# Attention and MLP on one core: group 0 brought in by strips of tokens, and a second product set between score tiles

## The chip, the cores and the metric

The kernel runs on one core of one Trainium2 chip. The metric is the device time of one execution in microseconds, as the median of several executions. The kernel before takes 394.6 us (three runs, 394.51 to 395.38). "Span" is the time from the first to the last instruction in a profile, some 1.8 us less. All runs used here are fast (one run of the kernel before, of 435.94 us, was slow and is left out).

## The reference

Sigmoid attention on 8 batches of 12 heads (448 tokens, 64 wide), then a two-layer MLP with GELU on the 3584 x 768 result:

```python
scores = scale * np.matmul(q, k.transpose(0, 1, 3, 2)) - np.log(S)
attn = 1.0 / (1.0 + np.exp(-scores))
x = matmul(attn, v)            # then heads side by side: 3584 x 768
h = x @ w_in                   # 768 x 2048
g = 0.5 * h * (1.0 + np.tanh(c * (h + 0.044715 * h * h * h)))
out = g @ w_out                # 2048 x 768
```

## The kernel before

The program is written by a planner: a small simulation in the kernel's source starts operations on each engine when their inputs are ready *by its own estimates*, and the order that results is what the chip executes, with semaphores for the true dependences. So the order of instructions on an engine is fixed once built. If a transfer is later on the chip than in the plan, the engine waits at that place, even if work behind it is ready.

A group is four heads of a batch (24 groups in all). Its q and k (448 KB each) are loaded as fp32, cast to bf16, transposed on TensorE into PSUM and copied to SBUF. Each group has 7 score tiles (four 64x64 matmuls of 448 columns, run at once in the quarters of the array), each followed by a sigmoid on ScalarE, or, after the first 21 tiles, by a tanh on ScalarE and an affine step on VectorE. A second product multiplies the 7 tiles with v (28 matmuls). PSUM has eight banks; a score tile takes a pair of them, a second product takes two, and a group of MLP matmuls takes one.

The planner's choice for TensorE while the MLP has work:

```python
whole = m > 0 and state["avj"] + m == NJ          # all 7 tiles of a group are ready
if pl.pe_mode == 64 and n >= UB and whole and (av_open or banks >= 2):
    ops = av_take(m, t)                           # the second product, right behind a burst
    state["queue"] = ops[1:]
    return ops[0]
size = min(can, banks // 2, free_pairs(t))
if size == BURST or size and hungry or ...:       # BURST = 3 score tiles
    ops = [make_qk(n + x, t) for x in range(size)]
    ...
# else a group of the MLP's first or second layer (make_a, make_b)
```

The loads of group 0 were halves of the partition-major data (`c` = 0, 1), two on SyncE's queue for k and two on ScalarE's for q; GpSimd's queue (v, later groups as bf16, weights) waits for the first half of k:

```python
first[nm] = [plan.add(Op("ld%s0.%d" % (nm, c), "SP" if nm == "k" else "AQ",
                         lambda e, c=c, ap=ap, d=dst[0]: e.dma_start(d[:, c, :], ap[:, c, :]), ...
# casts: k on VectorE, q on ScalarE, one per half; all 7 transposes of k, then of q; copies on both
```

## Time and profile before

| | before |
|---|---|
| device time, median of three | 394.64 us |
| TensorE busy | 98% of 392.7 us |
| first score tile begins | 7.52 us |
| first full MLP group begins ("MLP begins" below) | 29.91 us |
| from there to the end, no wait of TensorE in the records | 362.78 us |

Numbers that no view prints, such as the 362.78, are differences of the starts of single instructions in the same traces.

### The profile page before, as it was taken

The page shows a single profiled execution, that of the slowest core. Times are in us where ns is not written, and L with a number is a line of the kernel's source. Part 1 is how long each engine was busy: PE and PEld are TensorE (multiplying, and loading weights), DVE is VectorE, ACT ScalarE, POOL GpSimd, SP SyncE. Part 2 cuts the span into 40 slices and gives each one's busy share as a digit, 9 for nine tenths or more (in the row PEclk, how much of TensorE's full clock was granted, in tenths as well). Part 3 has the DMA queues.
Part 4 walks back from the last instruction along what each step waited for, and adds up shares of the span by engine and source line. Part 5 has one row for each costly group of instructions (what it writes and reads, how often), then busy time and mean ns, then how long its engine had stood idle before and what let it go on. Part 6 is the DMA issues. An engine that isn't in the chain of part 4 may idle for free.

```text
span 392.7 us, 7379 instructions
## 1 busy us (share of the span) xinstructions
PE 383.5 (98%) x3162; PEld 199.4 (51%) x3162; DVE 142.6 (36%) x243; ACT 237.0 (60%) x366; POOL 50.5 (13%) x82
## 2 busy tenths in 40 slices
PE   7799999999999999999999999999999999999996
PEld 3334455545545454555555555555554555555563
DVE  3347623147635672645443524434432400000000
ACT  5999963588667876857556665565747532333221
POOL 6992110011101201110110100110000000000000
PEclk9999999999999999999999999999999999999999
DMA  8999999657946895895647729637211011111133
GB/s 235 185 201 204 210 203 301 135 143 130 281 85 159 169 240 142 112 242 125 146 109 161 192 14 182 175 68 182 48 42 42 1 42 40 42 40 42 40 82 80
DMA packets 63521, 51.74 MB, mean 132 GB/s; under 512 B 36224, under 2 KB 60032, under 8 KB 63488
## 3 DMA queue, kind: packets, MB, share of 16 engines
q1 hardware_dynamic: 48320, 36.61, 38.3%
q0 software_dynamic: 14528, 13.64, 22.4%
q10 hardware_dynamic: 640, 1.02, 0.7%
q8 instruction: 25, 0.41, 0.4%
q14 instruction: 8, 0.07, 0.1%
HBM read 45.61 MB, written 11.01 MB: 144 GB/s over the span
## 4 chain that ended last, share of the span: by engine, by line
PE 94%; ACT 4%; DMA 1%; issue 0%; DVE 0%; SPq 0%
PE ps L715 38%; PE ps L753 37%; PE ps L581 9%; PE ps L628 8%; ACT at L592 3%; DMA kf<-in_k_dram 1%; PE ps L541 1%; PE ps L538 0%; ACT th L600 0%; ACT L596 0%; PE ps L403 0%; DVE kb L350 0%; ACT ob L349 0%; SPq L454 0%; ACT warm L596 0%
## 5 line engine op out<-in xcount | busy, mean ns | idle before, releaser
L715 PE MATMUL ps<-xT,w_in 128*128 128x448 bf16 x756 | 153.2, 353 | 0.0
L753 PE MATMUL ps<-w_out,gT 128*128 128x384 bf16 x896 | 152.9, 326 | 0.0
L604 DVE TENSOR_SCALAR at<-th 128x896 bf16<-128x896 f32 x147 | 90.5, 625 | 123.0 <-ACT th L600 122.8
L600 ACT ACTIVATE th<-ps 128x896 f32<-128x896 f32 x147 | 127.5, 928 | 0.6 <-PE ps L581 0.6
L753 PEld LDWEIGHTS ps<-w_out,gT 128*128 128x128 bf16 x896 | 86.8, 98 | 62.2 <-issue 2.5
L715 PEld LDWEIGHTS ps<-xT,w_in 128*128 128x128 bf16 x756 | 70.6, 98 | 75.0 <-issue 7.2
L729 ACT ACTIVATE gT<-ps 128x448 bf16<-128x448 f32 x128 | 70.6, 554 | 47.3 <-PE ps L715 47.2
L349 ACT ACTIVATE ob<-ps 128x384 f32<-128x384 f32 x56 | 27.5, 491 | 98.2 <-PE ps L753 98.2
L581 PE MATMUL ps<-qT,kT 64*64 64x448 bf16 x672 | 46.0, 359 | 3.6 <-ACT at L592 3.2
L474 POOL DMA_DIRECT2D vb<-in_v_dram x24 | 14.5, 605 | 213.5 <-PE ps L581 210.5
L628 PE MATMUL ps<-at,vb 64*64 64x448 bf16 x672 | 38.9, 351 | 0.0
L350 DVE CAST xT<-ps 128x448 bf16<-128x448 f32 x42 | 24.5, 619 | 19.8 <-PE ps L628 19.8
L581 PEld LDWEIGHTS ps<-qT,kT 64*64 64x64 bf16 x672 | 15.2, 105 | 30.8 <-issue 14.6
L628 PEld LDWEIGHTS ps<-at,vb 64*64 64x64 bf16 x672 | 20.8, 106 | 13.2 <-issue 7.1
L350 DVE CAST kb<-kf 128x896 bf16<-128x896 f32 (+1 forms) x21 | 13.2, 630 | 15.6 <-DMA kf<-in_k_dram 15.5
L592 ACT ACTIVATE at<-ps 128x896 bf16<-128x896 f32 x21 | 17.4, 935 | 0.8 <-PE ps L581 0.6
L476 POOL DMA_DIRECT2D vb<-in_v_dram x24 | 17.0, 708 | 0.2 <-issue 0.2
L350 DVE CAST qb<-qf 128x896 bf16<-128x896 f32 x19 | 11.9, 625 | 11.7 <-DMA qf<-in_q_dram 11.7
L808 POOL DMA_DIRECT2D w_in<-in_moe_w_in_dram x16 | 9.9, 659 | 0.0
L403 PE MATMUL ps<-gT,ident 128*128 128x512 bf16 x14 | 4.8, 501 | 1.5 <-POOL ident L357 1.5
L350 DVE COPY kT<-ps 128x896 bf16<-128x896 bf16 (+1 forms) x6 | 3.5, 591 | 3.5 <-PE ps L541 1.8
L349 ACT ACTIVATE xT<-ps 128x448 bf16<-128x448 f32 x6 | 3.4, 559 | 1.9 <-PE ps L628 1.9
(30 smaller groups left out, 36.4 us busy)
## 6 DMA issues: line engine op xcount, KB each, us to landing
out_dram<-ob SPq DMA_DIRECT2D x54, 192.0 KB, 2.7
kf<-in_k_dram SPq DMA_DIRECT2D x19, 448.0 KB, 4.3
qf<-in_q_dram SPq DMA_DIRECT2D x18, 448.0 KB, 5.8
vb<-in_v_dram POOLq DMA_DIRECT2D x48, 112.0 KB, 5.4
w_in<-in_moe_w_in_dram POOLq DMA_DIRECT2D x16, 192.0 KB, 10.7
w_out<-in_moe_w_out_dram POOLq DMA_DIRECT2D x4, 768.0 KB, 23.0
kb<-in_k_dram POOLq DMA_DIRECT2D x4, 224.0 KB, 8.6
qb<-in_q_dram POOLq DMA_DIRECT2D x4, 224.0 KB, 9.1
```

The costliest lines, as they stand in the source:

```text
L349: return e.activation(o, i, AF.Copy)
L350: return e.tensor_copy(o, i)
L474: a = plan.add(Op("ldv%da" % g, "SWQ", lambda e, d=dst[0:64], ap=lo: e.dma_start(d, ap), deps, 610.0, 0.0, prio=order_v(g), sem="ldv%da" % ...
L476: c = plan.add(Op("ldv%db" % g, "SWQ", lambda e, d=dst[64:128], ap=hi: e.dma_start(d, ap), deps, 610.0, 0.0, prio=order_v(g), sem="ldv%db" ...
L581: r = mm(ps[64 * half:64 * half + 64, (x, y)[a], 0:S], kv[d, a, j, :], qv[d, a, :, :], start=True, stop=True)
L592: lambda e: e.activation(at[as_][:], both, AF.Sigmoid, bias=bias, scale=scale),
L600: lambda e: e.activation(th[ts][:], both, AF.Tanh, bias=0.5 * bias, scale=0.5 * scale),
L604: lambda e: e.tensor_scalar(at[as_][:], th[ts][:], 0.5, 0.5, op0=ALU.mult, op1=ALU.add),
L628: r = mm(ps[64 * c:64 * c + 64, banks[a], 0:S], vb[s][d, slot, j, :], at[as_][d, a, :], start=(j == 0), stop=(j == NJ - 1))
L715: r = mm(ps[:, bank, 0:S], w_in[:, kt, fc * 128:(fc + 1) * 128], xT[xb][:, kt, :], start=(kt == 0), stop=(kt == KT - 1))
L729: lambda e: e.activation(gT[:, fc, col:col + S], ps[:, bank, 0:S], AF.Gelu_apprx_tanh),
L753: r = mm(ps[:, bank, 0:EH], gT[:, fc, col:col + 128], w_out[:, fc, half * EH:(half + 1) * EH], start=(fc == 0), stop=(fc == FC - 1))
```

## The change

Its intent: begin the sigmoids earlier, by bringing group 0 in as two parts (strips 0 to 3 and 4 to 6 of the seven 64-token strips), so that k's first part and q can be cast, transposed and used while k's second part is still coming; and let a second product no longer wait for the bank that the MLP has just left.

```diff
-        plan.free["ACT"] += 3 * 460.0
+        plan.free["ACT"] += 460.0
...
-                    first[nm] = [plan.add(Op("ld%s0.%d" % (nm, c), "SP" if nm == "k" else "AQ", ... d[:, c, :], ap[:, c, :]
+                    for x, (lo, hi) in enumerate(CUTS):                      # ((0, 4), (4, 7))
+                        ld[(0, x)] = plan.add(Op("ld%s0.%d" % (nm, x), "AQ" if (nm, x) == ("q", 0) else "SP",
+                              ... d[:, :, lo * D:hi * D], ap[:, :, lo * D:hi * D] ...
-                ld[g] = plan.add(Op("ld%s%d" % (nm, g), "AQ" if (nm, g) == ("q", 1) else "SP",
+                ld[g] = plan.add(Op("ld%s%d" % (nm, g), "SP",
...                                  # casts, transposes and copies of group 0 by the same parts
-            banks = [take(t), take(t)]
+            banks = list(take_pair(t)) if free_pairs(t) else [take(t), take(t)]
...
-            if pl.pe_mode == 64 and n >= UB and whole and (av_open or banks >= 2):
-                ops = av_take(m, t) ...
+            if state["more"]:
+                state["more"] -= 1
+                if pl.pe_mode == 64 and qk_ready(t, n) and free_pairs(t):
+                    state["n"] += 1
+                    return make_qk(n, t)
...
+                if whole and size == BURST and not av_open:
+                    size -= 1                # two tiles, the second product, then one more
+                    state["more"] = MORE
```

The warm-up matmuls also go from 512 to 256 columns each.

More of the change, by code (lines that the diff above doesn't have):

```diff
@@ L315, in bass_sigmoid_attention__then__act_gelu_tanh_kernel @@
     HBANKS = 2
+    MORE = 1
     SIG = 1
@@ L394, in give @@
             bank_busy[i] = False
-        blank = plan.add(Op("blank", "DVE", lambda e: e.memset(gT[:, 0, 0:512], 0.0), [], 200.0, 300.0, prio=(0, -2)))
+        blank = plan.add(Op("blank", "DVE", lambda e: e.memset(gT[:, 0, 0:256], 0.0), [], 200.0, 300.0, prio=(0, -2)))
         def make_warm():
@@ L402, in fn @@
             def fn(e):
-                return mm(ps[:, bank, :], ident[:], gT[:, 0, 0:512], start=True, stop=True)
-            op = Op("warm", "PE", fn, [eye, blank, bank_free[bank]], 225.0 if plan.now > 5500.0 else 435.0, 165.0, mode=128)
+                return mm(ps[:, bank, 0:256], ident[:], gT[:, 0, 0:256], start=True, stop=True)
+            op = Op("warm", "PE", fn, [eye, blank, bank_free[bank]], 113.0 if plan.now > 6000.0 else 218.0, 165.0, mode=128)
             give(bank, op)
@@ L426, in flat4 @@
             return t[b, 4 * i:4 * i + 4].rearrange("h s d -> (h s d)")
-        first = {}
+        CUTS = ((0, NJ // 2 + 1), (NJ // 2 + 1, NJ))
         def low_load(nm, g):
@@ L452, in load_qk @@
                 if g == 0:
-                    first[nm] = [plan.add(Op("ld%s0.%d" % (nm, c), "SP" if nm == "k" else "AQ",
-                                             lambda e, c=c, ap=ap, d=dst[0]: e.dma_start(d[:, c, :], ap[:, c, :]),
-                                             [], 460.0, 0.0, prio=(2, 0), sem="ld%s0.%d" % (nm, c), pkt=(8, 80.0)))
-                                 for c in range(2)]
-                    ld[g] = first[nm][1]
+                    for x, (lo, hi) in enumerate(CUTS):
+                        ld[(0, x)] = plan.add(Op("ld%s0.%d" % (nm, x), "AQ" if (nm, x) == ("q", 0) else "SP",
+                                                 lambda e, ap=ap, d=dst[0], lo=lo, hi=hi: e.dma_start(
+                                                     d[:, :, lo * D:hi * D], ap[:, :, lo * D:hi * D]),
+                                                 [], 460.0, 0.0, prio=(2, -2 if (nm, x) == ("k", 0) else -1 if nm == "q" else 0),
+                                                 sem="ld%s0.%d" % (nm, x), pkt=(16, 89.0 * (hi - lo) / NJ)))
+                    ld[g] = ld[(0, 1)]
                     continue
-                ld[g] = plan.add(Op("ld%s%d" % (nm, g), "AQ" if (nm, g) == ("q", 1) else "SP",
+                ld[g] = plan.add(Op("ld%s%d" % (nm, g), "SP",
                                     lambda e, ap=ap, d=dst[s]: e.dma_start(d[:], ap),
@@ L470, in load_v @@
             dst = vb[s][:].rearrange("p s j d -> p s (j d)")
-            deps = later(av, g - NVB) + (first["k"][:1] if g == 0 else [])
+            deps = later(av, g - NVB) + ([ld_k[(0, 0)]] if g == 0 else [])
             if g >= PE_TR * NG:
@@ L489, in cast_qk @@
                 if g == 0:
-                    who = {"k": "DVE", "q": "ACT"}[nm]
-                    half = [plan.add(Op("cast%s0.%d" % (nm, c), who,
-                                        lambda e, c=c, o=o_ap, i=i_ap, w=who: copy(e, o[:, c, :, :], i[:, c, :, :], w),
-                                        [first[nm][c]], 360.0, 500.0, prio=(0, -1))) for c in range(2)]
-                    cast[g] = half[1]
+                    for x, (lo, hi) in enumerate(CUTS):
+                        who = "ACT" if (nm, x) == ("q", 0) else "DVE"
+                        cast[(0, x)] = plan.add(Op("cast%s0.%d" % (nm, x), who,
+                                                   lambda e, o=o_ap, i=i_ap, w=who, lo=lo, hi=hi: copy(
+                                                       e, o[:, :, lo:hi, :], i[:, :, lo:hi, :], w),
+                                                   [ld[(0, x)]], (hi - lo) * 100.0, (hi - lo) * 110.0 + 150.0,
+                                                   prio=(0, -9 if nm == "q" or x == 0 else -1)))
+                    cast[g] = cast[(0, 1)]
                     continue
@@ L506, in transpose_qk @@
                 if g < PE_TR * NG:
-                    trans.append((g, nm, src[s], dst[st], cast, tr, freed, after))
+                    for x in range(2) if g == 0 else (None,):
+                        trans.append((g, nm, src[s], dst[st], cast, tr, freed, after, x))
+                    if len(trans) == 4 and g == 0:
+                        trans.append(trans.pop(1))
                     continue
@@ L517, in trans_ready @@
                 return False
-            if trans[0][0] == 0 and not free_pairs(t):
-                return False
-            g, nm, src, dst, cast, tr, freed, after = trans[0]
-            return g in cast and cast[g].end is not None and cast[g].end <= t
+            g, nm, src, dst, cast, tr, freed, after, x = trans[0]
+            key = g if x is None else (g, x)
+            return key in cast and cast[key].end is not None and cast[key].end <= t
         def make_trans(t):
-            g, nm, src, dst, cast, tr, freed, after = trans.pop(0)
-            banks = list(take_pair(t)) if g == 0 else [take(t)]
-            prev = [bank_free[x] for x in banks]
+            g, nm, src, dst, cast, tr, freed, after, x = trans.pop(0)
+            key = g if x is None else (g, x)
+            bank = take(t)
             flat = src[:].rearrange("p j c d -> p (j c d)")
-            to = [ps[:, x, 0:NJ * 64].bitcast(BF16) for x in banks]
-            cut = NJ // 2 + 1 if g == 0 else NJ
+            to = ps[:, bank, 0:NJ * 64].bitcast(BF16)
+            lo, hi = (0, NJ) if x is None else CUTS[x]
             low = low_load(nm, g)
@@ L534, in fn @@
                 r = None
-                for j in range(NJ):
-                    o = to[j // cut][:, 128 * j:128 * j + 128]
+                for j in range(lo, hi):
+                    o = to[:, 128 * j:128 * j + 128]
                     if not low:
@@ L543, in fn, with qk_needs @@
                 return r
-            freed[g] = op = Op("trp%s%d" % (nm, g), "PE", fn, [eye, cast[g]] + prev, NJ * 56.0, 165.0, mode=12864 if low else 128)
-            flat_o = dst[:].rearrange("p j x -> p (j x)")
-            if g == 0:
-                two = []
-                for x, (lo, hi, w) in enumerate(((0, cut * 128, "DVE"), (cut * 128, NJ * 128, "ACT"))):
-                    two.append(plan.add(Op("trc%s%d.%d" % (nm, g, x), w,
-                                           lambda e, x=x, lo=lo, hi=hi, w=w: copy(e, flat_o[:, lo:hi], to[x][:, lo:hi], w),
-                                           [op], 330.0, 450.0, prio=(0, -1))))
-                    give(banks[x], two[x])
-                tr[g] = All(two)
-                return op
-            tr[g] = plan.add(Op("trc%s%d" % (nm, g), "ANY",
-                                lambda e, who: copy(e, flat_o, to[0], who),
-                                [op] + after, 0, 0, prio=(0, g),
-                                alts={"DVE": (560.0, 680.0)}))
-            give(banks[0], tr[g])
-            return op
+            freed[key] = op = Op("trp%s%s" % (nm, key), "PE", fn, [eye, cast[key], bank_free[bank]],
+                                 (hi - lo) * 56.0 * (2 if t < 6000.0 else 1), 165.0, mode=12864 if low else 128)
+            flat_o = dst[:].rearrange("p j x -> p (j x)")[:, 128 * lo:128 * hi]
+            if (nm, x) == ("q", 0) or (nm, x) == ("k", 1):
+                alts = {"ACT": ((hi - lo) * 107.0 + 50, (hi - lo) * 107.0 + 190)}
+            else:
+                alts = {"DVE": ((hi - lo) * 70.0 + 70, (hi - lo) * 70.0 + 190)}
+            tr[key] = plan.add(Op("trc%s%s" % (nm, key), "ANY",
+                                  lambda e, who: copy(e, flat_o, to[:, 128 * lo:128 * hi], who),
+                                  [op] + after, 0, 0, prio=(0, g) if x is None else (0, -9), alts=alts))
+            give(bank, tr[key])
+            if x == 1:
+                tr[g] = All([tr[(g, 0)], tr[(g, 1)]])
+                freed[g] = All([freed[(g, 0)], freed[(g, 1)]])
+            return op
+        def qk_needs(g, j):
+            if g:
+                return [tr_q.get(g), tr_k.get(g)]
+            return [tr_q.get((0, 0)), tr_q.get((0, 1)), tr_k.get((0, 0 if j < CUTS[0][1] else 1))]
         def by_half(t):
@@ L584, in fn @@
                 return r
-            qk[(g, j)] = op = Op("qk%d.%d" % (g, j), "PE", fn, [tr_q[g], tr_k[g]] + prev,
+            qk[(g, j)] = op = Op("qk%d.%d" % (g, j), "PE", fn, qk_needs(g, j) + prev,
                                  4 * 2.5 + S / 2.4, 165.0, mode=64)
@@ L817, in load_w_out @@
                                        after, 760.0, 0.0, prio=prio, sem="wo%d" % n, pkt=(32, 117.0)))]
-        state = {"n": 0, "av": 0, "queue": [], "a": (0, 0), "b": 0, "h": 0, "avj": 0, "loaded": 0}
+        state = {"n": 0, "av": 0, "queue": [], "a": (0, 0), "b": 0, "h": 0, "avj": 0, "more": 0}
         def load(g):
@@ L857, in qk_ready @@
             g, j = units[n]
-            if g not in tr_q or n >= NAT and units[n - NAT][0] not in av:
+            if n >= NAT and units[n - NAT][0] not in av:
                 return False
-            return all(d.end is not None and d.end <= t for d in (tr_q[g], tr_k[g]))
+            return all(d is not None and d.end is not None and d.end <= t for d in qk_needs(g, j))
         def units_done(g, t):
@@ L930, in pe_next @@
             whole = m > 0 and state["avj"] + m == NJ
-            if pl.pe_mode == 64 and n >= UB and whole and (av_open or banks >= 2):
-                ops = av_take(m, t)
-                state["queue"] = ops[1:]
-                return ops[0]
+            if state["more"]:
[3 more added lines that the diff above has]
+                    return make_qk(n, t)
             size = min(can, banks // 2, free_pairs(t))
```

## The prediction

> **What bounds the kernel now.** I read the page first, then the waits of TensorE, then its instructions in order of time, and last the first 8 us on all engines. One core runs, its clock is granted in full, and TensorE is busy nearly all the time:
>
> ```profile
> span 392.7 us, 7379 instructions
> PE 383.5 (98%) x3162; PEld 199.4 (51%) x3162; DVE 142.6 (36%) x243; ACT 237.0 (60%) x366; POOL 50.5 (13%) x82
> ```
>
> The view of waits, for TensorE alone and the whole span, has only four lines, 5.4 us together, and asked from 60 us on it has none:
>
> ```profile
> PE ps L581 <- ACT at L592: 3.2, 10, 0.8
> PE ps L403 <- POOL ident L357: 1.5, 1, 1.5
> PE ps L538 <- DVE kb L350: 0.4, 1, 0.4
> PE ps L541 <- ACT th L600: 0.3, 1, 0.3
> ```
>
> So there are two stages. Up to about 29 us the kernel is bound by what feeds TensorE: first the load, cast, transpose and copy of group 0 (7.5 us), then a row of 21 sigmoids on ScalarE, then an activation table load. From about 30 us to the end TensorE never waits in the records. But a matmul's end is modelled, and ends overlap the next start, so short stalls don't show as waits. They show when the start of one run of matmuls is taken from the start of the next. This is the timeline of TensorE around one second product (L628; L581 is the score tiles, L715 and L753 the two layers of the MLP):
>
> ```profile
> 122.81 0.76 PE L581 MATMUL ps<-qT,kT 64*64 64x448 bf16 x12
> 123.55 1.52 PE L628 MATMUL ps<-at,vb 64*64 64x448 bf16 x28
> 125.00 2.44 PE L715 MATMUL ps<-xT,w_in 128*128 128x448 bf16 x12
> 127.38 0.76 PE L581 MATMUL ps<-qT,kT 64*64 64x448 bf16 x12
> 128.07 2.77 PE L753 MATMUL ps<-w_out,gT 128*128 128x384 bf16 x16
> ```
>
> A burst of three score tiles (12 matmuls, four at a time in quarters of the array) takes 128.07 - 127.38 = 0.69 us to the next MLP matmul, mode switch included. When a second product follows, the same three tiles take 123.55 - 122.81 = 0.74 us to a run in the *same* mode, where no switch is due. Without any wait it should be shorter than 0.69, not longer. ScalarE tells what is waited for: the copy of the last MLP result out of PSUM.
>
> ```profile
> 122.92 0.49 ACT L349 ACTIVATE ob<-ps 128x384 f32<-128x384 f32 x1 [1.82 <-PE ps L753]
> ```
>
> It ends at 123.41, 0.14 us before the second product's first matmul at 123.55. Three score tiles take six of the eight PSUM banks and the second product the other two, one of which is the one that this copy is still emptying. One place in the kernel before already has the order that the change makes the rule (two tiles, second product, one tile):
>
> ```profile
> 36.29 0.57 PE L581 MATMUL ps<-qT,kT 64*64 64x448 bf16 x8
> 36.69 1.49 PE L628 MATMUL ps<-at,vb 64*64 64x448 bf16 x28
> 38.01 0.36 PE L581 MATMUL ps<-qT,kT 64*64 64x448 bf16 x4
> ```
>
> with the MLP's next matmul at 38.30. The start of the kernel:
>
> ```profile
> 4.23 0.62 DVE L350 CAST kb<-kf 128x448 bf16<-128x448 f32 x1 [3.06 <-DMA kf<-in_k_dram]
> 5.51 0.58 ACT L349 ACTIVATE qb<-qf 128x448 bf16<-128x448 f32 x1 [0.51 <-DMA qf<-in_q_dram]
> 6.50 0.49 ACT L349 ACTIVATE kT<-ps 128x384 bf16<-128x384 bf16 x1 [0.41 <-PE ps L538]
> 6.89 0.42 DVE L350 COPY qT<-ps 128x512 bf16<-128x512 bf16 x1
> 7.52 0.57 PE L581 MATMUL ps<-qT,kT 64*64 64x448 bf16 x8
> 7.95 4.33 ACT L592 ACTIVATE at<-ps 128x896 bf16<-128x896 f32 x5 [0.57 <-PE ps L581]
> ```
>
> The last half of q lands at 5.5, and the first score tile, which needs all of q and k, starts at 7.52, the first sigmoid at 7.95.
>
> **What the Trainium skill says.** "TensorEngine Tiling (Array Packing)", section Key Properties: changing the tiling mode drains TensorE. The trace agrees: 16 second-layer matmuls take 2.60 us before a first-layer run but 2.70 before a score burst (chain of waits), and three score tiles that should take 0.57 take 0.69 before the MLP; so each excursion costs about 0.1 us on either side; the change makes no new excursion, since all three parts of the new burst are in one mode. "TensorE: Matmul & The Clock Gate", section "Wait — 56ns, not 53.3ns?": start to start is N/2.4 GHz plus some 2.5 ns, 189 ns for 448 columns. The trace agrees: 28 matmuls in fours, 1.32 us from 36.69 to 38.01, are 189 ns per four. "Perfetto Trace Analysis", section Matmuls: independent groups should rotate through PSUM banks so that the evacuation of one overlaps the next; the 0.14 us are a place where that fails. "VectorE: DVE Perf Modes", section Mode 2×_2P: the double rate splits the access pattern along its outermost dimension. The trace fits with this:
>
> ```profile
> L350 DVE CAST kb<-kf 128x896 bf16<-128x896 f32 x19 | 12.0, 631 | 12.1 <-DMA kf<-in_k_dram 12.1
> L350 DVE CAST kb<-kf 128x448 bf16<-128x448 f32 x2 | 1.2, 620 | 3.4 <-DMA kf<-in_k_dram 3.4
> ```
>
> Half the elements take the same time. The halves of before have 7 strips as outermost dimension, the whole tile has 2; a part by strips has 2 again. I take from this, as an estimate, that the new casts go at the fast rate. No run yet shows that the odd 7 is the reason.
>
> **Part 1, the burst.** Before: 0.74 + 1.45 = 2.19 us from the first score tile to the MLP. After, by the starts at 36.29, 36.69, 38.01 and 38.30: 0.40 + 1.32 + 0.29 = 2.01. The saving is 0.18 us. The second product takes the third free pair of banks, the emptied bank is wanted only 1.7 us after the burst begins (by the third tile), when the copy has long ended (0.6 us after). I counted in the timeline how often 12 matmuls of L581 are directly followed by 28 of L628: 17 times, at 87 to 308 us, every one with 0.74. 17 x 0.175 (the unrounded starts) = 3.0 us. All of it lies on TensorE where nothing else is waited for, so all of it reaches the end. A second product that isn't ready when a burst begins is now put off to the next burst; by the end of the last `at` tile before each burst that concerns 1 of 17 (104.25, ready 0.3 us after its burst began), and it still gets its place in a burst, so it costs nothing unless it ends up alone (about 0.2 us for a mode change in and out).
>
> **Part 2, the start.** Bytes of group 0 stay the same, 917 KB, all landed by 5.5. Their order changes: four of seven strips of k and of q first (262 KB each, against 229 before, landed at 4.2 and 4.4), then the rest of q, then of k. 66 KB more at some 390 GB/s (the rate of the DMA view from 2.7 to 6.9 us) put the first parts at 4.4 and 4.6, the rest of q at about 5.0, of k at 5.5. Packets shrink from 1,792 to 1,024 and 768 bytes, which may cost 0.1.
> - k part 0: cast on VectorE 4.4 to 4.85 (512 elements at (631/896) ns are 0.36, plus a fixed part, 0.43), four transposes at 56 ns, copy after q's cast, 5.4 to 5.8.
> - q part 0: cast on ScalarE, 0.58 + 64 elements more at 0.83 ns = 0.63, to 5.25; transposed by 5.55; copy of 512 on ScalarE, 0.6, 5.7 to 6.3.
> - q part 1: cast on VectorE 5.0 to 5.4, transposed by 5.75, copied 5.9 to 6.25.
>
> The first score tile then starts at 6.3 + 0.2 (before, 0.2 passed from the last copy's end at 7.31 to 7.52) = 6.5, 1.0 us earlier. k part 1 is copied on ScalarE, 0.49 long and 0.4 from start to start; if it comes behind the first sigmoid, ScalarE, which bounds this stage, loses 0.4 of the gain. So 0.6 to 1.0, and I take 0.8. ScalarE's row then runs on unhindered: group 1 was needed at 10 us and later, its q load moves behind k's on one queue and may land half a us later.
>
> **Sum.** 394.64 - 3.0 - 0.8 = 390.8; I say 390.9, 1.0% less.
>
> **Rivals.**
> - *The wait only moves.* The third tile, or the MLP after the burst, finds no free bank. For it: eight banks, all in use in a burst. Against: the first tile's tanh ends about 1.4 us after the burst begins (123.31 + 0.91 = 124.22 against 122.81), the MLP returns at 2.0. If it were so, part 1 would give nothing: 393.8.
> - *The order of work shifts.* The instruction order comes from a planner that reacts to every moved time. A burst dropped to two tiles, or a second product alone, costs 0.2 each; three more would take 0.6, three fewer give it. For it: the kernel before has two products outside full bursts. 390.3 to 391.5.
> - *The start is bound elsewhere.* The loads' smaller packets, or q's second part stuck behind others on one queue, keep the first tile at 7.3; or weights hold the MLP. Against the latter: the first weights have landed by 23 us and the MLP proper begins at 29.9. It would make 391.6.
> - *Two per cent.* A gain of 7.9 us would need the MLP's matmuls themselves (306 us) to shrink; nothing touches them.
>
> **Range and chances.** The first part is measured inside the same trace, so its doubt is the count (15 to 19, 2.6 to 3.3 us); the second is 0.3 to 1.0, the planner adds 0.6 either way. That gives 389.7 to 392.2. Faster by over 2% (below 386.7) 0.03, within 2% 0.95, slower by over 2% (above 402.5) 0.02: the last only if the new order stalls everywhere.
>
> **What would show it.** In the changed timeline: bursts of 8, 28 and 4 with 0.40, 1.32 and 0.29 between starts, some 17 of them, and no 12 followed by 28; the first score tile near 6.5 and the first sigmoid near 6.9; VectorE casts of 512 elements near 0.43 us; no new waits of TensorE after 30 us. It is wrong if the 28 still begin late, if single tiles are left over as bursts of their own, or if the start's gain is gone by 30 us.

## The result, and the profile after

| | before (6 runs) | after (6 runs) |
|---|---|---|
| median | 394.84 us | 392.04 us |
| all runs | 394.51 to 395.38 | 391.87, 391.96, 392.01, 392.07, 392.24, and 394.74 |

The ratio of the fast runs is 0.9939, with a 95% interval of 0.9913 to 0.9966. Executions over 1.5% slower than the fastest of the same kernel are left out of the means. Ratios here are the mean time of one kernel's fast runs over that of the other's of the same rounds, so they aren't quite the ratio of the medians. The gain is 2.4 us by this ratio (0.0061 x 394.8), where 3.7 were predicted. The one run of 394.74 is the profiled one, and it is the slow one of two kinds: its granted clock is 0.990, that of the others 0.999 or 1.0.

The second half of the prediction's picture is as told. TensorE's timeline of the changed kernel (start, duration, engine, line, operation; L591 score tiles, L638 second product, L725 and L763 the MLP's layers):

```profile
124.33 0.57 PE L591 MATMUL ps<-qT,kT 64*64 64x448 bf16 x8
124.73 1.49 PE L638 MATMUL ps<-at,vb 64*64 64x448 bf16 x28
126.06 0.36 PE L591 MATMUL ps<-qT,kT 64*64 64x448 bf16 x4
126.35 2.44 PE L725 MATMUL ps<-xT,w_in 128*128 128x448 bf16 x12
```

From the first score tile to the MLP it is 126.35 - 124.33 = 2.02 us for three tiles and a second product, as predicted (2.01, before 2.19). No burst of 12 is followed by 28 any more; 19 have the new form. From the begin of the MLP to the end it is 360.46 us instead of 362.78.

The first half isn't as told. The same view at the start, of TensorE and then of ScalarE:

```profile
7.73 0.57 PE L591 MATMUL ps<-qT,kT 64*64 64x448 bf16 x8
...
10.00 0.93 PE L545 MATMUL ps<-ident,kb 128*128 128x128 bf16 x7 [1.70 <-DVE kb L351]
10.86 0.96 PE L591 MATMUL ps<-qT,kT 64*64 64x448 bf16 x8
```
```profile
8.16 1.73 ACT L602 ACTIVATE at<-ps 128x896 bf16<-128x896 f32 x2 [0.24 <-PE ps L591]
11.50 1.73 ACT L602 ACTIVATE at<-ps 128x896 bf16<-128x896 f32 x2 [1.61 <-PE ps L591]
```

The first tile comes at 7.73 and not at 6.5. After two tiles TensorE stands until 10.00 (in brackets the idle time and what ended it: the cast of k, here of group 1), since group 1's transposes are next in its order; ScalarE, which bounds this stage, has two sigmoids to do and then nothing for 1.6 us. Before, seven sigmoids followed each other from 7.95 without such a hole. And from 10.00 on seven transposes take 0.93 instead of 0.56 us: TensorE runs at half clock. The view by windows (time, then busy us and count for TensorE, its weight loads, VectorE, ScalarE, GpSimd, then the granted clock, DMA share and GB/s):

```profile
6.25:9.66 3.41, 1.45 (x17) 0.51 (x14) 1.56 (x4) 2.56 (x4) 3.41 (x6) 1.00 1.14 245
9.66:16.49 6.83, 6.13 (x62) 3.09 (x62) 2.06 (x4) 4.36 (x6) 6.83 (x11) 0.50 1.21 187
```

The MLP begins at 32.45 us in this profile, 2.5 us *later* than before. What the late data are is in the DMA view of the first 12 us (output and input, queue, count, size, us from issue to landing). Before, then after:

```profile
kf<-in_k_dram SPq DMA_DIRECT2D x1, 448.0 KB, 5.8
qf<-in_q_dram ACTq DMA_DIRECT2D x1, 448.0 KB, 6.5
```
```profile
kf<-in_k_dram SPq DMA_DIRECT2D x1, 448.0 KB, 7.0
qf<-in_q_dram SPq DMA_DIRECT2D x1, 448.0 KB, 7.6
kf<-in_k_dram SPq DMA_DIRECT2D x1, 192.0 KB, 4.6
```

Group 1's loads are the whole ones of 448 KB. Issued at 1.7 us they landed at 7.5 and 8.2; issued at 2.3 and 2.8, behind three parts on one queue, they land at 9.3 and 10.4. Also k's second part of group 0 lands at 1.76 + 4.6 = 6.35 us where the whole of group 0 had landed by 5.5.

So the theory at this point: (A) the bursts give the whole gain and the start gives none, since group 1 lands late (A1: it is the single queue, which GpSimd's loads starve once they move at 7 us; A2: it is the smaller packets), and since TensorE, standing still, is put to half clock in some executions. Rival (B): the start gives its 0.8 us, and only the half clock hides it.

### The profile page after: what moved, and what is told of

Same layout as the page of the kernel before. It is cut to its first block, busy times and chain, and to the rows that moved or that the text cites.

```text
span 392.9 us, 7405 instructions
## 1 busy us (share of the span) xinstructions
PE 383.2 (98%) x3168; PEld 200.9 (51%) x3168; DVE 133.3 (34%) x228; ACT 242.6 (62%) x381; POOL 50.7 (13%) x82
## 4 chain that ended last, share of the span: by engine, by line
PE 93%; ACT 3%; DMA 2%; DVE 0%; SPq 0%; issue 0%
PE ps L725 38%; PE ps L763 37%; PE ps L591 9%; PE ps L638 8%; ACT at L602 2%; DMA kf<-in_k_dram 2%; PE ps L548 1%; PE ps L545 0%; ACT th L610 0%; SPq L456 0%; ACT L606 0%; DVE kb L351 0%; DVE kT L351 0%; DVE qb L351 0%; ACT ob L350 0%
## 5 line engine op out<-in xcount | busy, mean ns | idle before, releaser
L725 PE MATMUL ps<-xT,w_in 128*128 128x448 bf16 x756 | 153.2, 353 | 0.0
L763 PE MATMUL ps<-w_out,gT 128*128 128x384 bf16 x896 | 153.1, 326 | 0.0
L610 ACT ACTIVATE th<-ps 128x896 f32<-128x896 f32 x147 | 129.7, 928 | 0.7 <-PE ps L591 0.7
L763 PEld LDWEIGHTS ps<-w_out,gT 128*128 128x128 bf16 x896 | 86.7, 98 | 62.4 <-issue 2.9
L725 PEld LDWEIGHTS ps<-xT,w_in 128*128 128x128 bf16 x756 | 70.6, 98 | 74.8 <-issue 7.4
L591 PE MATMUL ps<-qT,kT 64*64 64x448 bf16 x672 | 50.3, 367 | 1.9 <-ACT at L602 1.5
L638 PE MATMUL ps<-at,vb 64*64 64x448 bf16 x672 | 39.4, 356 | 0.0
L591 PEld LDWEIGHTS ps<-qT,kT 64*64 64x64 bf16 x672 | 15.3, 106 | 28.5 <-issue 15.2
L638 PEld LDWEIGHTS ps<-at,vb 64*64 64x64 bf16 x672 | 19.9, 109 | 12.2 <-issue 1.5
L351 DVE CAST xT<-ps 128x448 bf16<-128x448 f32 x26 | 15.8, 618 | 14.2 <-PE ps L638 14.2
L351 DVE CAST kb<-kf 128x896 bf16<-128x896 f32 (+2 forms) x21 | 12.9, 613 | 16.1 <-DMA kf<-in_k_dram 16.0
L351 DVE CAST qb<-qf 128x896 bf16<-128x896 f32 (+1 forms) x20 | 12.2, 609 | 11.5 <-DMA qf<-in_q_dram 11.5
L350 ACT ACTIVATE xT<-ps 128x448 bf16<-128x448 f32 x22 | 12.2, 561 | 1.9 <-PE ps L638 1.9
L404 PE MATMUL ps<-gT,ident 128*128 128x256 bf16 x20 | 4.3, 398 | 1.5 <-POOL ident L358 1.5
```

The source lines that it names most:

```text
L350: return e.activation(o, i, AF.Copy)
L351: return e.tensor_copy(o, i)
L591: r = mm(ps[64 * half:64 * half + 64, (x, y)[a], 0:S], kv[d, a, j, :], qv[d, a, :, :], start=True, stop=True)
L610: lambda e: e.activation(th[ts][:], both, AF.Tanh, bias=0.5 * bias, scale=0.5 * scale),
L638: r = mm(ps[64 * c:64 * c + 64, banks[a], 0:S], vb[s][d, slot, j, :], at[as_][d, a, :], start=(j == 0), stop=(j == NJ - 1))
L725: r = mm(ps[:, bank, 0:S], w_in[:, kt, fc * 128:(fc + 1) * 128], xT[xb][:, kt, :], start=(kt == 0), stop=(kt == KT - 1))
```

## The experiments

Fourteen runs were made, each with five rounds against the kernel before, all correct. They come in four sets, each set on another chip, so times of different sets are compared with care. "MLP begins" and "MLP to end" are from the profile of each. One run, the kernel before against itself, shows the noise: 394.9 us, ratio 0.9991 (0.9971 to 1.0012); in its profile the first tile begins at 7.64 and MLP to end is 362.79 us.

### The changed kernel again, twice

No edit. 

> The changed kernel once more, unedited, for a profile at full clock (the first one fell into a run in which TensorE's clock was granted at half from 9.7 to 16.5 us). Theory A (the bursts give all of the gain, the start gives nothing): 392.0 us, 0.9925 to 0.994 of before; in a full-clock profile TensorE stops after the second score tile at about 8.3 us until group 1's k has landed and been cast at about 10 us, ScalarE idles some 2 us there, and the MLP proper starts at 29.6 to 30.2 us, where it started before (29.9). Rival B (the start gives 0.8 us and the half clock alone hid it): MLP from 29.0 us or earlier in a full-clock run.

 

> The changed kernel a third time, for its profile at full clock and for how often it drops to half clock (3 of 12 executions so far: 394.5 to 394.8 us, against 391.7 to 392.7 for the others). At full clock: first score tile near 7, stop of TensorE of about 2 us before group 1's transposes, MLP proper at 29.4 to 30.0.

Measured: 392.32 us (391.69 to 394.79), ratio 0.9954, and 392.21 us (391.48 to 393.54), ratio 0.9927. Both profiles fell in executions with the half clock again. Of all 18 executions of the changed kernel, 13 have a granted clock of 0.998 or more and take 391.5 to 392.7 us, 392.0 on average; the other five, at 0.990 to 0.996, take 393.0 to 394.8, 394.1 on average. None of the 49 fast executions of the kernel before in these sets of rounds (43 beside other kernels, 6 against itself) is below 0.998 (they take 394.95 us on average). MLP to end is 360.45 and 360.47 us in these profiles: all of the difference between executions lies before the MLP. At full clock that leaves 390.2 - 360.45 = 29.75 us for the start (390.2 is the median span of those executions), against 393.1 - 362.78 = 30.3 for the kernel before: a gain of 0.55 us there, not 0.8, and the changed order of work gives it back: the stage behind takes 0.62 us more than with the bursts alone (359.83 us, next run). So at full clock too the start brings nothing in all, and rival B falls. Within the same rounds the changed kernel at full clock is 0.30 us faster than the bursts alone in one set (392.05 against 392.35) and 0.25 slower in the other (392.00 against 391.75).

### The burst alone, twice

```diff
 # the kernel before, with only: MORE, state["more"], take_pair for the second product,
 # the removed block behind a burst, and size -= 1
```

> The kernel before with the new burst alone. Theory A: all of the gain is here: 391.9 to 392.3 us, ratio to before 0.992 to 0.9945, that is 2.4 to 3.0 us, from some 17 to 19 second products that no longer begin 0.14 us late; the start as before (first score tile at 7.5, MLP proper at 29.9). Rival B: 0.8 us less gain than with both parts, some 392.9 us.

 

> The burst alone once more, to see whether its start, which is the start of the kernel before to the instruction, is really 0.6 us later on average, or whether that was the moment at which the clock was released (7.1 us in that profile, 4.5 in the profile of before). If it was that moment: 391.5 to 392.4, on average 2.4 to 2.9 us under before; from the first MLP group to the end 359.8 again.

Measured: 392.37 us (391.53 to 393.22), ratio 0.994, and 391.77 us (391.38 to 392.18), ratio 0.9909. No execution is at half clock. MLP to end is 359.83 us both times, 2.95 less than before; 18 bursts have the new form (two of its four lines here, 2.02 us apart):

```profile
87.98 0.57 PE L582 MATMUL ps<-qT,kT 64*64 64x448 bf16 x8
...
90.00 2.44 PE L716 MATMUL ps<-xT,w_in 128*128 128x448 bf16 x12
```

The averages of the two sets (392.35 and 391.75) differ by 0.6; they ran on two chips, and the second set's ratio is helped by two long runs of the kernel before (396.33 and 397.2). The start of this kernel is that of the kernel before to the instruction; its profiles differ by when the clock was released (7.12 and 6.11 us) and begin the first tile at 8.26 and 7.77; the kernel before, released at 4.45 and 5.03, begins it at 7.52 and 7.64. So the moment of release is worth up to 0.7 us of scatter from one execution to the next. Over both sets it is 392.05 us on average, 0.6 less than the changed kernel (392.6 over its 18). The burst is the gain.

### The start alone

```diff
 # the changed kernel, with the five edits of the burst undone
```

> The kernel before with the new start alone. Theory A: 394.4 to 395.2 us, no change: the first score tile doesn't start before 7.3 us, TensorE waits for group 1's k until about 10 us, and the 17 bursts of three tiles with a second product still take 2.19 us. Rival B: 393.8 to 394.2 us. If the half clock comes at all in this and not in e2, it comes from the idle time of TensorE between 8 and 10 us; such an execution is 2.5 to 3 us longer.

Measured: 396.42 us (394.49 to 396.87), ratio 1.0031 (1.0010 to 1.0051): slower than before. Two executions at full clock take 394.49 and 394.57, no gain to speak of; four at 0.990 to 0.995 take 396.1 to 396.9. The old bursts are back in its timeline with 2.19 us. So the start by itself is worth nothing at full clock and costs 2 us at half.

### Group 1's q back on ScalarE's queue

```diff
-                ld[g] = plan.add(Op("ld%s%d" % (nm, g), "SP",
+                ld[g] = plan.add(Op("ld%s%d" % (nm, g), "AQ" if (nm, g) == ("q", 1) else "SP",
```

> The changed kernel with group 1's q load back on ScalarE's queue (one word of the change undone). Theory A1 (the one queue that now holds 1.57 MB is still moving 0.2 MB when the loads of GpSimd's queue begin to move at 7 us, and those starve it): with two queues group 1's k and q land at 7.5 to 8.5 instead of 9.3 and 10.4, TensorE's stop after the second tile is gone or below 0.7 us, and the time is 391.0 to 391.7. Rival A2 (the smaller packets are what delays it): group 1 lands at 9 or later still, and the time stays at 391.8 to 392.2.

Measured: 392.29 us (392.17 to 392.79), ratio 0.994; no half clock. Group 1's q lands at 6.66 instead of 10.4, its k at 8.74; but k's second part of group 0, now sharing the engines with that q, lands only at 7.22, and the first tile begins at 8.04. The stop after the second tile is 0.84 us, no more than in the kernel before (0.83), and the time is that of the changed kernel at full clock: the wait moved ahead of the first tile. The expected 391.0 to 391.7 was a miss.

### GpSimd's loads held until group 1's k has landed

```diff
-            deps = later(av, g - NVB) + ([ld_k[(0, 0)]] if g == 0 else [])
+            deps = later(av, g - NVB) + ([lambda: ld_k.get(1)] if g == 0 else [])
```

> The changed kernel with the first load of GpSimd's queue (v of group 0, and all behind it) held until group 1's k has landed, instead of the first part of group 0's k. Theory A1 (the one hardware queue is starved from 7 us on by GpSimd's loads): group 1's k lands near 7.2 and its q near 7.8 instead of 9.3 and 10.5, TensorE's stop after the second score tile falls from 2.3 us to below 0.6, no execution drops to half clock, and with the start's gain kept the time is 391.0 to 391.7; the later weights may take some of it back. Rival A2 (the queue is slow by its small packets): group 1 lands after 8.5 all the same, and the time doesn't move from 391.7 to 392.3.

Measured: 393.4 us (392.81 to 394.74), ratio 0.9966: worse. Group 1 lands at 8.07 and 9.20, where the changed kernel's own three profiles have 8.27 to 9.29 and 9.68 to 10.52; in the run with both remedies (below) it lands at 7.67 and 8.79. So starving has a part in it, 0.5 to 0.9 us for q against the earliest of the three, but the landing of before (7.5 and 8.2) doesn't come back. All the same, the sigmoids now run without a hole:

```profile
8.04 17.75 ACT L602 ACTIVATE at<-ps 128x896 bf16<-128x896 f32 x21 [0.25 <-PE ps L591]
```

The hole after the second sigmoid is gone: all 21 sigmoids stand in one row. It begins later than before, though, so that the 21st begins at 24.86 us where it was 24.70 in the kernel before. TensorE has a new wait in the list:

```profile
PE ps L701 <- DMA w_in<-in_moe_w_in_dram: 1.0, 1, 1.0
```

The weights, held back with the rest of GpSimd's queue, come 1 us too late, and v with them, so that less of the fixed work of TensorE is done in its idle time before the MLP (more transposes and second products lie behind its begin). That is how I read it; no run takes these two apart. Two executions dropped to 0.991 and 0.995 all the same.

### TensorE's order changed, loads left alone; and both remedies

```diff
+            if g == 1 and state["n"] < FIRST:      # FIRST = 7: group 1's transposes behind group 0's tiles
+                return False
...
-                if m and not soon:
+                if m and not soon and n >= FIRST:  # second products behind them too
```

> The changed kernel with the loads left alone, but in TensorE's order group 1's transposes and all second products come behind the seven score tiles of group 0. Theory C (the late landing costs only because the transposes stand in TensorE's fixed order ahead of tiles that are ready): ScalarE's idle time before its sigmoids falls from 2.7 to some 0.5 to 1 us, TensorE has no stop of 2 us, hence no half clock; 390.6 to 391.3. Rival: ScalarE needs group 1 itself by then (seven sigmoids of 0.8 us end at 13 us, and q's transposes are copied at 13 us), and nothing is won: 391.7 to 392.3 without the slow executions.

 

> Both remedies, the order and the held loads. If A1 and C are two views of the same loss, this gives no more than the better of them (390.6 to 391.5); if they are two losses, it is below both by 0.4 us or more. The weights land 2 us later than in the changed kernel; if the MLP needs them at its begin, the time goes back to 392.

 

> Group 1's q on ScalarE's queue again and GpSimd's loads held as in the run before. Theory A1: group 1 lands by 7.5 in both, but the second part of group 0's k lands at about 7 as in the run with the queue alone (7.2), since two queues share the engines, so the first score tile stays near 7.8; 391.5 to 392.2, no half clock. Rival: two queues move more bytes in all, all lands by 7.0, 391.0 to 391.5.

Measured: 394.55 us (ratio 0.9987) with the order, 394.58 us (0.9992) with order and held loads, 393.91 us (0.9974) with held loads and q on ScalarE's queue. All three expectations are missed. The order does what it should at first: seven sigmoids in a row from 7.89 us. Then the edit's own fault shows: the planner put the five second-product steps that I had held back into the place after the transposes, ahead of the next tile, and at half clock.

```profile
7.89 5.78 ACT L605 ACTIVATE at<-ps 128x896 bf16<-128x896 f32 x7 [0.48 <-PE ps L594]
16.73 2.54 ACT L605 ACTIVATE at<-ps 128x896 bf16<-128x896 f32 x3 [3.06 <-PE ps L594]
```

With a hole of 3 us in another place this run doesn't decide whether the order alone would do; that stays open. It has one use: all six of its executions are below 0.997 of the clock, although in the profiled one no gap of TensorE in the 3.41 us before the drop is longer than 1.45 us: it was busy for 1.52 of them, with gaps of 1.45 and 0.43 us and then a tile every 0.8 us.

### The six first loads dealt to two queues

```diff
-  "AQ" if (nm, x) == ("q", 0) else "SP"
+  "AQ" if (nm, x) in (("q", 0), ("k", 1)) else "SP"      # and group 1's q on AQ
```

> The changed kernel with its six first loads dealt evenly to two queues: k part 0, q part 1 and group 1's k on SyncE's; q part 0, k part 1 and group 1's q on ScalarE's (the strips and the bursts stay). Theory A1 (what spoils the start is that group 1, and k part 1, come late on one queue): group 0 complete by 5.7, group 1 by 7.5 and 8.2 as before the change, first score tile at 6.6 to 7.0, no stop of TensorE above 0.8 us, no execution at half clock, MLP proper near 29.2; 391.2 to 391.7 in all executions. Rival A2 (packets of 768 and 1,024 bytes are slow): group 1 lands after 8.5 and the time stays at 391.8 or above.

Measured: 391.78 us (391.23 to 393.3), ratio 0.9914; one of six executions at 0.996. Group 1 lands at 8.59 and 9.35 and group 0 complete at 6.15, not at 5.7: late as before the edit, with two queues and the same packets. TensorE's stop is 0.75 us. The first tile begins at 7.75, not at 6.6 to 7.0; in this profile the clock was released only at 7.50. The time is inside the scatter of the changed kernel. The expectation for the landings was missed, and the rival's came true: it is not mainly the queue.

### The old packets on the new queues

```diff
-  d[:, :, lo * D:hi * D], ap[:, :, lo * D:hi * D]       # runs of 1,024 and 768 bytes
+  d[:, x, :], ap[:, x, :]                               # runs of 1,792 bytes, as before
-  [ld[(0, x)]], (hi - lo) * 100.0
+  [ld[(0, 0)], ld[(0, 1)]], (hi - lo) * 100.0           # a cast waits for both halves
...                                                      # and the planner's estimate of these loads
```

> The changed kernel with group 0's four loads in whole runs of 1,792 bytes again (two halves, on the same queues in the same order), so the packets of before on the queues of after; casts wait for both halves. Rival A2 (small packets delay the queue): group 1's k lands before 8.2 and its q before 9.2. Theory A1 (one queue, and what is left on it at 7 us is starved): group 1 lands at 9.0 or later and 10.0 or later as in the changed kernel (9.3 and 10.5); the first score tile starts later than in the changed kernel, at about 7.5, as its casts wait for more bytes; time 391.8 to 393.

Measured: 391.84 us (391.39 to 392.39, four runs), ratio 0.9924, none at half clock. On the same queues in the same order, group 1 now lands at 6.79 and 8.42:

```profile
kf<-in_k_dram SPq DMA_DIRECT2D x1, 448.0 KB, 4.6
qf<-in_q_dram SPq DMA_DIRECT2D x1, 448.0 KB, 5.8
```

Six profiles have the changed kernel's loads as they are (three of itself, the start alone, the changed order, and the filled one below): k lands at 8.10 to 9.29, q at 9.68 to 10.52. Against the earliest of them both come 1.3 us sooner here, in the one profile taken. TensorE's stop after the second tile falls to 0.3 us, and six sigmoids follow each other from 7.87. A2 is right for the main part, and A1 for the smaller one that the held loads showed. The first tile begins at 7.43, as expected, since the casts wait for all bytes; so the strips bring nothing this way, but they cost nothing either: MLP begins at 29.78, and from there to the end it is 359.82, as with the burst alone.

### Idle matmuls in TensorE's stop

```diff
+  def make_fill():      # ten matmuls of 256 columns in front of each transpose of group 1
+      ...
```

> The changed kernel with ten idle matmuls of 256 columns (1.1 us at full clock) put in front of each of group 1's two transposes, where TensorE stops for 1 to 2.3 us anyway. Theory H (the half clock follows a stretch of 3.41 us in which TensorE was busy for 1.6 us or less): no execution drops to half clock, so none is above 393 us, and the average falls from 392.6 to 391.8 to 392.2; the stop itself stays. Rival: the clock goes by something else (the length of the gap, chance), and again about 5 of 18 executions are above 393 us with a granted clock of 0.997 or less.

Measured: 392.71 us (392.32 to 394.54), ratio 0.9957. No execution is below 0.998 of the clock, so the first part of the expectation held; in the profile the window ahead is full:

```profile
7.13:10.54 3.41, 3.36 (x40) 2.10 (x39) 1.47 (x4) 2.62 (x4) 3.41 (x6) 1.00 1.16 206
```

Six of six is no proof by itself: with a chance of 13 in 18 each it would happen in one of seven such sets. The second part failed: two executions at full clock take 393.54 and 394.54. What made them slow isn't known, as they weren't profiled; the landing of group 1 is a candidate, and fill of 1.1 us is in the way whenever the data come early.

## Why the prediction was wrong

**What bounds the kernel: right.** Two stages, and every microsecond saved on TensorE after the MLP's begin reached the end.

**Part 1, the burst: right, in mechanism and size.** Predicted 17 x 0.175 = 3.0 us; the burst alone measures 362.78 - 359.83 = 2.95 in that stage, twice, and 2.02 us per burst where 2.01 was predicted. The prediction read the cause, the copy out of the bank, from one burst; in the trace of the kernel before all 17 second products begin 0.143 or 0.144 us behind the end of such a copy. This 0.14 is the way from the copy to the matmul (0.14 also lies between the last copy and the first tile); the wait is the 0.17 us that the three tiles take beyond their own 0.57. In the full change it is 2.3, since the planner's order shifted by 0.62 us: one more pair of transposes lies behind the MLP's begin (0.91 instead of 0.51), which is 0.40 of it, and there are 52 visits to the 64-wide mode instead of 51, more of them with two tiles or one. The prediction had this as its rival "the order of work shifts" with 0.6 either way, and it came out at the bad end.

**Part 2, the start: wrong.** The step that failed is "ScalarE's row then runs on unhindered: group 1 was needed at 10 us and later, its q load moves behind k's on one queue and may land half a us later". Both halves of it fail. Group 1's transposes of k come right behind the second tile in TensorE's order and were due at 8.3 us in the changed kernel, not at 10 (even in the kernel before, behind a third tile, they began at 9.24); and its q landed 1.5 to 2.4 us later and its k 0.8 to 1.8 us later. What the loads cost was put down as "may cost 0.1" for the packets; with only the packets undone (the run with whole runs of 1,792 bytes) group 1 comes 1.3 us or more earlier. The first tile, at 7.0 to 7.7 us in the three profiles instead of 6.5, is late for the same reason: k's second part landed at 5.9 to 6.4 instead of 5.5, and work on it stands ahead of the first tile in the fixed orders. On VectorE its cast comes before the two last copies that the first tile needs:

```profile
6.38 0.62 DVE L351 CAST kb<-kf 128x384 bf16<-128x384 f32 x1 [0.65 <-DMA kf<-in_k_dram]
6.92 0.40 DVE L351 COPY kT<-ps 128x512 bf16<-128x512 bf16 x1
7.25 0.34 DVE L351 COPY qT<-ps 128x384 bf16<-128x384 bf16 x1
```

The last copy ends at 7.59 (6.89 and 7.22 in the other two profiles), and the first tile begins 0.14 to 0.15 us behind it in all three. The prediction had these copies done at 5.8 and 6.25. On TensorE the transposes of k's second part stand ahead of the tile too; I had set them behind it. (A smaller misreading: before the change the last copy ended at 7.38, on ScalarE, and not at 7.31.) So of the predicted 0.8 us only 0.55 came, at full clock, and the shift of order told under part 1 takes that back.

**What wasn't in it at all: the half clock.** In 5 of 18 executions TensorE's clock is halved for 3.4 or 6.8 us (seen in the three profiled ones, and by the granted clock of the other two), which costs 2.1 us each (394.1 against 392.0), on average 0.6. It follows a window in which TensorE was busy too little: the seven such profiles (three of the changed kernel, the start alone, the changed order with and without held loads, and q back with held loads) show 1.07 to 1.72 busy us in the 3.41 before, while all windows that kept the clock among those looked at have 2.2 or more (2.22 with GpSimd's loads held, 2.29 in the kernel before, 3.36 in the filled one). That the idleness causes it is shown so far as these windows and the filled run go; where between 1.72 and 2.22 the limit lies isn't known. Nor is it decided that the busy time is what counts: the longest gap within the window parts the same windows, 1.03 us or more where the clock fell and 0.95 or less where it stayed, and the filled run took away both. Once halved, the clock stayed so behind windows with 2.5 to 2.8 busy us (four profiles) and came back behind a full 3.41 (all seven).

**The sum**, then: -2.95 for the bursts, +0.62 for the order, -0.55 for the start, +0.6 for the half clock, -2.3 us on average. Measured over all 18 executions: 392.6 against 394.95, -2.3. The predicted sum was -3.8; the bursts account for all of it that came.

**The rivals.** "The wait only moves" was wrong: no wait of TensorE after the MLP begins. "The start is bound elsewhere" was right for its first reason, the loads' smaller packets, which it priced at nearly the whole 0.8 us but to which it gave too little weight. Its other reason, weights that hold the MLP, came true only when they were held back on purpose.

**The casts: right.** The working assumed 0.43 us for a cast of 512 elements on VectorE, by the outermost dimension of 2 instead of 7. The changed kernel's list of instructions has it:

```profile
4.50 0.43 DVE L351 CAST kb<-kf 128x512 bf16<-128x512 f32 x1 [3.46 <-DMA kf<-in_k_dram]
5.37 0.36 DVE L351 CAST qb<-qf 128x384 bf16<-128x384 f32 x1 [0.44 <-DMA qf<-in_q_dram]
```

This step held and saved 0.2 us, on a part of the path that then waited for data. That the odd 7 was the reason is not shown: no run changes it alone.

**What stays open.** How packets of 1,024 and 768 bytes in place of packets of 1,792 bytes delay the group behind them by 1.3 us or more: their own durations in the trace (medians of 46, 36 and 74 ns) account for 2 x 256 x (46 + 36 - 74) ns over 16 engines = 0.26 us. In the changed kernel the last 0.2 MB of the queue trickle from 7 to 10 us, beside GpSimd's loads, while in the run with whole packets the queue is nearly empty at 7.5. The loss begins before that: from 3 to 7 us the core's DMA moves 331 to 352 GB/s in the six profiles with the changed loads, 334 and 341 with GpSimd's loads held, 370 with the loads dealt to two queues, 379 with whole packets on the one queue, and 394 to 400 in the four profiles with the loads of before. So against whole packets 0.1 to 0.2 MB more is left at 7 us, when GpSimd's packets set in. The packets' own durations account for 0.1 MB of it (0.26 us at 390 GB/s); why what is left then takes until 9 or 10 us to land isn't shown, nor which of the 16 engines lagged.

## What to carry to other kernels

Take the start of one run of matmuls from the start of the next: a wait of 0.17 us for a PSUM bank, 17 times, that no list of waits shows was worth 3 us here, and work in the same array mode that needs no new bank is the thing to put in front of it. When loads are cut into pieces for an earlier start, look at what stands *behind* them on the queue and at what the consumer's fixed order will wait for; the first tile may come earlier and the fourth later. And price a new gap on TensorE twice: by its length, and by the half clock that it may bring. Of the kernels tried, the burst alone (392.05 us on average of 12, never at half clock) and the burst with whole packets (391.9, four runs) are better on average than the full change (392.6 of 18), and all of them better than the kernel before; the whole packets were never run in the same rounds as the other two.

## What the Trainium skill lacked or had wrong

- "TensorE: Matmul & The Clock Gate", section "HAM oscillation — how this bites in real kernels", gives the rule as no idle gaps of TensorE beyond some 3.4 us. Here the clock was halved behind gaps of 2.35 us at most, in three profiles of 1.03 to 1.05 us at most, where TensorE was busy for 1.07 to 1.72 us in the 3.41 us before; windows with 2.2 us or more, and gaps of 0.95 at most, kept it. The page has no figure for how busy such a window must be; whether the busy share or a shorter gap is the better rule isn't decided here.
- "DMA: Bandwidth & Descriptors", section "Why small descriptors are slow (HBM only)", gives a fixed cost per packet, by which (3 cycles on top of one for each 32 bytes) 768-byte packets are an estimated 7% slower per byte than those of 1,792 (9% with the 32 bytes of metadata that it also counts for each). The trace has 36 against 74 ns, 13% slower per byte, and the loads queued behind landed 1.3 us later or more; no run here shows where the rest of that delay comes from.
- "TensorEngine Tiling (Array Packing)", section Key Properties, says that changing mode drains the array but has no figure. Here it is 0.09 us going in (16 second-layer matmuls take 2.60 us to a first-layer run, 2.69 to a score burst) and 0.10 coming out (the single tile at a burst's end takes 0.29 us to the MLP, where a tile takes 0.19 within a run).
